# Masked Q for two heads in one K group, exp in steps of 3 and 2 banks, and zero-weight matmuls in TensorE's gaps

## Chip, cores and metric

The kernel runs on one core of a Trainium2 chip. The metric is the device time of one execution in microseconds (us). Each time quoted is a median over all of a kernel's executions, slow ones included. The program uses one core, so "slow" here only means that a run was over 1.5% above the fastest of its kernel.

Engine names in the profile: PE is TensorE (matmuls), PEld its weight loads, DVE is VectorE, ACT is ScalarE, POOL is GpSimd, SP issues the DMAs. QK stands for the score matmuls, PV for the product of the probabilities with V, and PSUM for the memory that TensorE writes its results to; the kernel uses it as eight banks of 512 fp32 columns.

## The reference, cut

One transformer block for 2048 tokens of width 512: layernorm, attention with 32 heads of 16, output projection, residual, layernorm, gated GELU FFN with 1792 hidden columns, residual. What matters here:

```python
scores = einsum("bhqd,bhkd->bhqk", q, k) * 16 ** -0.5
p = softmax(scores)            # 32 heads x 2048 x 2048 exponentials
o = einsum("bhqk,bhkd->bhqd", p, v)
h = x + (o merged) @ wo
h2 = h + (gelu(LN(h) @ w_gate) * (LN(h) @ w_up)) @ w_down
```

The 134 million exponentials run on ACT. They set the lower bound of the kernel.

## The kernel before, the parts that matter

Work is cut into 32 units: 4 chunks of 512 queries times 8 slots of 4 heads. A unit has 64 score tiles of 128 keys x 512 queries. A tile takes one PSUM bank. The four heads of a slot lie on the partitions 0, 32, 64 and 96, so QK matmuls with 32 rows each can run side by side in the array (in the trace those of one group start 0.003 us apart). Each head has 16 dimensions; the kernel pads each to 32 rows with zero weights.

A planner in the kernel's Python orders all instructions in advance from modelled durations. Each engine then runs its list in order and waits on semaphores.

```python
SLOTB = [(0, 1), (2, 3)]         # two slots of two banks for scores
PVB = 4                          # one bank accumulates P @ V
sch = Sched(P, [5, 6, 7])        # three banks for everything else ("dense")
def qk():                        # TensorE
    for st in range(NSTEP):      # 1024 steps of two banks
        yield Op("pe", 0.25, [two QK matmuls], gate=lambda: C["exp"] >= st - 1)
def exps():                      # ScalarE
    for st in range(NSTEP):
        yield Op("act", 0.9, ACTF(PT[:, p0:p0 + 2, :], pbank[:, bk[0]:bk[0] + 2, :], ACT.Exp), ...)
def pv():                        # TensorE, four matmuls side by side, then once a unit:
    ...                          # copy PVB out, transpose in fp32, normalise
```
(cut: reads, writes and ring indices)

Every eighth unit a query chunk is complete. Its output projection, second layernorm and FFN are then threaded between the exps of the next chunk. The FFN of the last chunk is the tail.

The planner makes an engine wait for its own earlier instruction whenever that one wrote the same buffer:

```python
def _waits_for(self, e, deps, extra=()):
    for (k, v) in list(deps) + list(extra):
        if k == e.name and v > e.count:   # only skips its own *current* group
            continue
        ...                               # else: wait on that semaphore, its own included
```

## Time and profile before

| | before |
|---|---|
| median time | 1202.06 us |
| span of the profiled run | 1193.7 us |
| mean granted TensorE clock | 0.707 |
| exps: first start, last end | 26.0 us, 1123 us |

The page, cut to the busy times, the granted clock in 40 slices of the span (in tenths of full speed), and the costliest groups (count, then busy us and mean ns of one, then idle time before them and its releaser):

```profile
PE 1072.0 (90%) x5442; PEld 268.1 (22%) x5499; DVE 277.8 (23%) x478; ACT 1019.5 (85%) x1102; POOL 189.5 (16%) x194
...
PEclk9799998555799955555589955555569965555589
...
L1131 ACT ACTIVATE PT<-pbank 128x1024 bf16<-128x1024 f32 x1024 | 983.5, 1023 | 99.0 <-PE pbank L1125 86.7
L1125 PE MATMUL pbank<-QT,KT 32*128 32x512 bf16 x2048 | 526.0, 519 | 80.7 <-ACT PT L1131 59.8
```

ACT is busy with exps nearly all the time, and where it isn't it waits for QK on PE. PE's clock is full only while there is dense work: the start, the three FFN stretches and the tail. Between them are quiet stretches with QK and PV alone, and there it is half.

Two quiet stretches in the windows view (start and end, length, busy time and count of each engine, granted clock, DMA):

```profile
450.00:510.00 60.00, 52.75 (x250) 11.04 (x248) 2.06 (x4) 58.03 (x62) 0.00 (x0) 0.50 0.00 1
700.00:760.00 60.00, 52.64 (x254) 11.31 (x252) 2.75 (x6) 57.27 (x62) 0.00 (x0) 0.50 0.00 1
```

PE is 88% busy here and still gets half clock. ACT is over 95% busy, so the half clock costs little. The timeline of such a stretch (start, length, engine, line, operation, count, idle before and releaser; PE only):

```profile
759.10 0.61 PE L1125 MATMUL pbank<-QT,KT 32*128 32x512 bf16 x2 [0.31 <-ACT PT L1131]
759.64 0.60 PE L1125 MATMUL pbank<-PT,VA 128*17 128x512 bf16 x4
```

From the QK pair's start to that of the PV group behind it is 0.54 us: this is what one group occupies at half clock. At full clock, in the FFN stretches of the same trace, it is 0.32 us.

### The profile page before, as it was taken

Reading aid. Unit: us, or ns where it says so; the run is one execution under the profiler, and the core shown is the slowest. Engines: PE = TensorE matmul, PEld = TensorE weight load, DVE = VectorE, ACT = ScalarE, POOL = GpSimd, SP = SyncE. Lnnn points to the kernel's source line nnn. Section 1 sums busy time; section 2 is a strip of 40 time slices with the busy share of each in tenths; the row PEclk is TensorE's granted clock in tenths of the full one; section 3 lists DMA queues with packets and bytes.
Section 4 is the critical chain, followed back from the end, with each engine's and each line's share of the span. In section 5 each row is a group of like instructions: output and inputs, shape, how many; then the busy total and the mean of one; then the engine's idle time right before and its main releaser. Section 6 shows DMA issues by size and latency. Waiting matters only on the chain.

```text
span 1193.7 us, 14797 instructions
## 1 busy us (share of the span) xinstructions
PE 1072.0 (90%) x5442; PEld 268.1 (22%) x5499; DVE 277.8 (23%) x478; ACT 1019.5 (85%) x1102; POOL 189.5 (16%) x194
## 2 busy tenths in 40 slices
PE   8899998888999988888999988888999988888887
PEld 2222222111222211111222211111222221111222
DVE  5343332000465100000356100000245300000232
ACT  4679999999888999999788999999889899999620
POOL 8500000000187000000059000000039200000000
PEclk9799998555799955555589955555569965555589
DMA  4000005000000100000000000000000000000000
GB/s 141 1 1 1 1 1 184 19 1 1 1 1 1 36 1 1 1 1 1 1 1 1 15 22 1 1 1 1 1 1 1 10 27 1 1 1 1 1 2 21
DMA packets 12848, 14.95 MB, mean 13 GB/s; under 512 B 1760, under 2 KB 11744, under 8 KB 12768
## 3 DMA queue, kind: packets, MB, share of 16 engines
q1 hardware_dynamic: 12768, 13.90, 3.5%
q8 instruction: 48, 0.79, 0.3%
q14 instruction: 32, 0.26, 0.1%
HBM read 11.80 MB, written 2.10 MB: 12 GB/s over the span
## 4 chain that ended last, share of the span: by engine, by line
PE 65%; issue 14%; ACT 14%; DVE 2%; POOL 1%; ACTq 0%; DVEq 0%
PE pbank L1125 39%; PE pbank L1124 20%; ACT PT L1131 13%; PE pbank L1323 3%; PE pbank L1365 2%; DVE OA L1319 1%; POOL xn_sb L1214 1%; PE pbank L1359 0%; PE pbank L1381 0%; ACT w_sb L1417 0%; ACTq L152 0%; DVE stats_93 L1372 0%; DVE w_sb L1418 0%; DVE QT L1254 0%; DVE h_c_69 L1368 0%
## 5 line engine op out<-in xcount | busy, mean ns | idle before, releaser
L1131 ACT ACTIVATE PT<-pbank 128x1024 bf16<-128x1024 f32 x1024 | 983.5, 1023 | 99.0 <-PE pbank L1125 86.7
L1125 PE MATMUL pbank<-QT,KT 32*128 32x512 bf16 x2048 | 526.0, 519 | 80.7 <-ACT PT L1131 59.8
L1125 PE MATMUL pbank<-PT,VA 128*17 128x512 bf16 x2048 | 270.1, 519 | 0.8 <-ACT PT L1131 0.6
L1125 PEld LDWEIGHTS pbank<-QT,KT 32*128 32x128 bf16 x2048 | 111.2, 96 | 503.6 <-PE pbank L1125 365.1
L1375 POOL TENSOR_SCALAR rstd_95<-mv_94 128x1 f32<-128x1 f32 x16 | 3.6, 222 | 907.2 <-DVE mv_94 L1373 907.2
L1319 DVE COPY OA<-pbank 128x512 f32<-128x512 f32 x32 | 22.1, 691 | 522.8 <-PE pbank L1125 522.8
L1125 PEld LDWEIGHTS pbank<-PT,VA 128*17 128x17 bf16 x2048 | 50.6, 89 | 187.1 <-issue 136.8
L1124 PE MATMUL pbank<-wd_sb,GUT 128*128 128x512 bf16 x213 | 59.2, 382 | 2.7 <-PE pbank L1125 1.0
L1411 POOL TENSOR_TENSOR w_sb<-w_sb,g_sb 128x512 f32<-128x512 f32 x42 | 56.7, 1351 | 3.5
L1409 POOL TENSOR_TENSOR w_sb<-g_sb 128x512 f32<-128x512 f32 x42 | 49.8, 1186 | 21.8 <-DVE g_sb L1407 21.7
L1323 PE MATMUL pbank<-ident_79,OA 128*128 128x128 f32 x128 | 38.9, 401 | 6.5 <-DVE OA L1319 5.7
L1418 DVE SCALAR_TENSOR_TENSOR w_sb<-w_sb,g_sb 128x512 f32<-128x512 f32 x42 | 41.9, 999 | 7.4 <-ACT w_sb L1417 7.3
L1423 ACT ACTIVATE w_sb<-pbank 128x512 f32<-128x512 f32 x14 | 8.4, 597 | 37.5 <-PE pbank L1124 37.5
L1124 PE MATMUL pbank<-xnT,wq_pad 128*128 128x512 bf16 x119 | 36.3, 384 | 1.6 <-PE pbank L1125 0.6
L1124 PE MATMUL pbank<-xnT,wk_pad 128*128 128x512 bf16 x121 | 36.6, 383 | 1.2 <-PE pbank L1125 0.5
L1407 DVE COPY g_sb<-pbank 128x512 f32<-128x512 f32 x42 | 29.0, 690 | 35.9 <-PE pbank L1124 35.8
L1443 DVE SCALAR_TENSOR_TENSOR GUT<-pbank,w_sb 128x512 bf16<-128x512 f32 x42 | 29.0, 691 | 24.5 <-PE pbank L1124 23.2
L1410 POOL TENSOR_SCALAR w_sb<-w_sb 128x512 f32<-128x512 f32 x42 | 30.5, 726 | 3.7
L1257 DVE CAST KT<-pbank 128x512 bf16<-128x512 f32 x32 | 22.1, 691 | 31.6 <-PE pbank L1124 31.6
L1254 DVE TENSOR_SCALAR QT<-pbank 128x512 bf16<-128x512 f32 x31 | 21.4, 689 | 34.1 <-PE pbank L1124 34.1
L1365 PE MATMUL pbank<-wo_sb,OnT 128*128 128x512 bf16 x57 | 24.9, 529 | 2.6 <-issue 1.7
L1417 ACT ACTIVATE w_sb<-w_sb 128x512 f32<-128x512 f32 x42 | 26.3, 626 | 0.0
(100 smaller groups left out, 484.5 us busy)
## 6 DMA issues: line engine op xcount, KB each, us to landing
xres<-in_A_x_dram SPq DMA_DIRECT2D x16, 128.0 KB, 2.3
out_dram<-out_sb SPq DMA_DIRECT2D x16, 128.0 KB, 1.7
wg_sb<-in_B_w_gate_dram SPq DMA_DIRECT2D x1, 1792.0 KB, 7.3
wu_sb<-in_B_w_up_dram SPq DMA_DIRECT2D x1, 1792.0 KB, 11.8
wd_sb<-in_B_w_down_dram SPq DMA_DIRECT2D x1, 1792.0 KB, 16.5
x_sb<-in_A_x_dram SPq DMA_DIRECT2D x3, 512.0 KB, 7.2
wqkv_sb<-in_A_wqkv_dram SPq DMA_DIRECT2D x2, 384.0 KB, 7.9
x_sb<-in_A_x_dram SPq DMA_DIRECT2D x2, 256.0 KB, 2.9
```

What stands on the lines that cost most here:

```text
L1124: return lambda e: e.matmul(o, l, r, start=start, stop=stop)
L1125: return lambda e: e.matmul(o, l, r, start=start, stop=stop, tile_position=tile)
L1131: return lambda e: e.activation(out=o, in_=i, func=func, **kw)
L1319: yield Op("dve", 0.61, lambda e: e.tensor_copy(out=OA[:, par, :], in_=pbank[:, PVB, :]), reads=[("pb", PVB)], writes=[("OA", par)])
L1323: yield Op("pe", 0.44, [lambda e, qt=qt: e.transpose(out=pbank[:, b, 128 * qt:128 * qt + 128], in_=OA[:, par, 128 * qt:128 * qt + 128], id ...
L1365: yield Op("pe", 0.44, [lambda e, hc=hc: e.matmul(pbank[:, b2, :], OnT[:, qt, hc, :], wo_sb[:, hc, :], start=(hc == 0), stop=(hc == 3)) fo ...
L1407: yield Op("dve", 0.61, lambda e: e.tensor_copy(out=gs, in_=pbank[:, b, :]), reads=[("pb", b)], writes=[("g", i)], extra=dE)
L1409: yield Op("pool", 1.05, lambda e: e.tensor_tensor(out=ws, in0=gs, in1=gs, op=ALU.mult), reads=[("g", i)], writes=[("w", i)])
L1410: yield Op("pool", 0.62, lambda e: e.tensor_scalar(out=ws, in0=ws, scalar1=GA, scalar2=1.0, op0=ALU.mult, op1=ALU.add), reads=[("w", i)], ...
L1411: yield Op("pool", 1.27, lambda e: e.tensor_tensor(out=ws, in0=ws, in1=gs, op=ALU.mult), reads=[("w", i), ("g", i)], writes=[("w", i)])
L1418: yield Op("dve", 0.6, lambda e: e.scalar_tensor_tensor(out=ws, in0=ws, scalar=1.0, in1=gs, op0=ALU.add, op1=ALU.mult), reads=[("w", i), ( ...
L1443: fn = lambda e: e.scalar_tensor_tensor(out=GUT[:, fc, :], in0=pbank[:, b, :], scalar=0.5, in1=w_sb[:, i, :], op0=ALU.mult, op1=ALU.mult)
```

## The change

Its intent: (1) fewer projections, because two heads share a 32-row K group and each Q copy is zero outside its own head; (2) fewer ACT instructions, 3 and 2 banks in turn; (3) full TensorE clock everywhere, by matmuls with zero weights ("fills") wherever the plan has a gap on PE. The banks now go 5 to scores, 1 to PV, 2 to dense work. The diff cut to its core:

```diff
-NRING = 20
+NRING = 30
+SLOTS = ((0, 3), (3, 2))
+PVB = 5
+DENSE = (6, 7)
+COLS = 3900
-    KT = at("KT", [128, NSLOT, S], BF16)
+    KT = at("KT", [128, 4, S], BF16)
 # K: one projection serves two slots; Q: one projection, two masked copies
-  op = ... tensor_scalar(out=QT[:, c, slot, :], in0=pbank[:, b, :], scalar1=0.25, ...)
+  for par in range(2):
+      ... tensor_scalar(out=QT[:, c, 2 * j + par, :], in0=pbank[:, b, :], scalar1=qmask[:, par:par + 1], ...)
 # QK and exp: a step is now n = 3 or 2 banks
-  ACTF(PT[:, p0:p0 + 2, :], pbank[:, bk[0]:bk[0] + 2, :], ACT.Exp)
+  ACTF(PT[:, p0:p0 + n, :], pbank[:, b0:b0 + n, :], ACT.Exp)
+    fill_op = Op("pe", TMM, lambda e: e.matmul(pbank[:, PVB, :], zero_bf[:], ones_bf[:], start=False, stop=False, ...), writes=[("pb", PVB)], cols=512)
+    def fill(st):                       # st: when PE's next real work is planned to start
+        if C["pv"] % NT and C["pv"] < NT * NU:
+            op = fill_op                # adds zero to the bank that PV accumulates in
+        elif sch.banks: ...             # or into a free dense bank
+        t0 = max(sch.t["pe"], sch._ready(op))
+        if st - t0 < TMM or sch.busy_columns(t0) >= COLS:
+            return False                # no gap, or 3900 columns planned in the last 3.4 us
+        sch._emit(op, t0)
```
(cut: durations of the model, keys, item lists, head order)

`busy_columns` counts a 512-column matmul on the full array as 512 and a QK matmul on 32 rows as 128. The order of the built kernel has 456 fills: 21 to 25 in each of the 16 quiet units (362 together), 14 to 23 in the unit before each run of them, 0 to 3 in each of the others, and 14 in the tail.

## The prediction

> **What bounds it now.** ScalarE, with stalls. The page has ACT busy 1019.5 of 1193.7 us, of which the 1024 exps (128x1024) are 983.5. In the trace they start every 0.92 us when nothing disturbs them: 1024 x 0.915 = 937 us. But the exps run from 26.0 to 1123.0 us, 1097 us. The missing 160 us, from start-to-start times of exps: about 20 before 90 us, 11 in the projections (90-190), 39 in the quiet units (mean 0.984, with 1.05 about one time in four and 1.5-1.7 where a unit ends and fp32 transposes run), and 85 in the three FFN stretches (22 of it are the 42 tanh between exps). The waits view names PE nearly alone: 86.7 us in 136 waits of exps on QK. The rest is the start (26 us) and the tail (71 us).
>
> The granted clock is 0.5 in all quiet stretches and for about 14-37 us into each FFN stretch; mean 0.707. Cold, a QK pair takes a slot of 0.53 us, warm 0.32. The Trainium skill (TensorE: Matmul & The Clock Gate, Part 1) says activity in windows of about 3.4 us releases the throttle; the trace agrees, its clock changes fall on multiples of 3.41 us. Weighting matmul columns by the share of the array used, I count about 1,850 per window in quiet stretches; windows kept or gained full clock from about 2,900 up.
>
> **What the change does.**
> 1. Exp of 3 and 2 banks. 0.915 = 0.062 + 2 x 0.4265, so five banks cost 2.257 us, not 2.288: 410 x 0.031 = 13 us less of pure ScalarE time. On the critical path, but small.
> 2. Fills. 456 zero matmuls by the instruction order, about 23 per quiet unit. With QK and PV that makes about 3,300 columns per window, enough on average but, as they come in clumps, not always; I expect some cold windows near unit ends. Warm PE: QK 26 x 0.33 + PV 16 x 0.33 + fills 23 x 0.3 = about 21 of 29 us, so fills fit. Gain: most of the quiet excess (39 to about 20), and each FFN stretch starts warm (non-tanh excess 63 to about 40).
> 3. Sharing K. Projections fall from 80 to 48: 128 matmuls of 0.22-0.27 us less, mostly before 195 us. Q is evacuated twice (0.69 us DVE each), K half as often. Start and projections: about 10 us.
> 4. Dense banks 3 to 2, PT ring 20 to 30. Neither should bind: DVE evacuations take 0.69 us, FFN is paced by POOL (about 3.3 us per gate). Tail, with seven free banks and a warm clock: 5 us better.
>
> **Sum.** Start 24 + exps 924 + tanh 22 + start/projection stalls 23 + quiet 22 + FFN 40 + tail 66 = 1121 if savings are partial; about 1075 if stalls nearly vanish. I predict 1100 us, 1060 to 1145. Faster by over 2%: 0.91; within: 0.05; slower: 0.04.
>
> **What would show it.** Granted clock in quiet stretches 0.85-1.0 (step 2). Exp pitch per five banks 2.26-2.32 us in quiet units (steps 1, 2), unit about 29.5 us against 31.5. PE-to-exp waits down from 87 to below 45 us. Tail at or below 67 us.
>
> **What would make it wrong.** Fills too few to hold the clock: they then run at half speed in front of QK and PE (about 2.6 us per five banks) becomes the bound: 1180-1250 us. Or full-array fills between row- and column-tiled groups costing a drain each, well over 0.3 us. Or two dense banks starving FFN so the tail grows.

## The result, and the profile after

The changed kernel takes **1262.71 us** (median of 4) against 1202.06 us: slower by 5.3%. Ratios in this document are the mean time of one kernel's fast runs over that of the other's in the same rounds, so not quite the ratio of the medians; here 1.053, with a 95% interval of 1.0475 to 1.0586.

The page after, same lines, and the fills:

```profile
PE 1138.9 (90%) x5723; PEld 276.7 (22%) x5827; DVE 259.5 (21%) x462; ACT 997.6 (79%) x897; POOL 181.7 (14%) x191
...
PEclk8899655555699995555689955555599985555599
...
L1151 ACT ACTIVATE PT<-pbank 128x1536 bf16<-128x1536 f32 (+1 forms) x819 | 959.3, 1247 | 180.6 <-PE pbank L1145 177.0
L1145 PE MATMUL pbank<-QT,KT 32*128 32x512 bf16 x2048 | 420.7, 509 | 44.0 <-ACT PT L1151 39.0
...
L1511 PE MATMUL pbank<-ones_bf,zero_bf 128*128 128x512 bf16 x386 | 226.6, 587 | 36.5 <-PE pbank L1145 21.3
```

The exps themselves took 24 us less (959.3 against 983.5), as they should. But they waited 177 us for QK instead of 86.7, the mean clock did not rise (0.708), and the fills ran at a mean of 587 ns. (Some matmul records are missing from a trace; the weight loads show all 456.)

Where the time went shows best by parts of the program. I take the start of each unit's first exp in the trace; "quiet" are the last four units of each chunk, "FFN" the first four units of chunks 1 to 3.

| us | start | units 0-3 | 12 FFN units | 16 quiet units | tail | span |
|---|---|---|---|---|---|---|
| before | 26.0 | 146.5 | 443.5 | 506.9 | 70.8 | 1193.7 |
| after | 30.1 | 136.9 | 407.3 | 616.8 | 68.9 | 1260.1 |

Outside the quiet units the change gained 44 us. In the quiet units it lost 110: 38.6 us each against 31.7. Three stretches with only QK, PV and fills, in the windows view:

```profile
150.00:210.00 60.00, 55.14 (x241) 11.33 (x242) 2.07 (x4) 47.22 (x41) 0.00 (x0) 0.50 0.00 1
435.00:465.00 30.00, 23.51 (x158) 6.77 (x160) 2.07 (x4) 30.00 (x28) 0.00 (x0) 1.00 0.08 23
750.00:810.00 60.00, 55.63 (x239) 11.23 (x242) 2.06 (x5) 47.02 (x41) 0.00 (x0) 0.50 0.00 1
```

The middle one is what the change was made for. The clock came out of the FFN at full and the fills kept it there for a while. ACT never stops (30.00 of 30.00 us). Five banks took 2.26 us between 430 and 468 us, where I had predicted 2.26 to 2.32. The other two show the state after the clock has been lost: it stays at half until the next dense work, and ACT works 47 of 60 us. Five banks take 3.05 us.

PE's timeline in the half-clock state:

```profile
229.15 0.61 PE L1145 MATMUL pbank<-PT,VA 128*17 128x512 bf16 x4
229.82 0.10 PEld L1511 LDWEIGHTS pbank<-ones_bf,zero_bf 128*128 128x128 bf16 x1 [0.58 <-PE pbank L1145]
229.83 1.27 PE L1511 MATMUL pbank<-ones_bf,zero_bf 128*128 128x512 bf16 x2
230.49 0.10 PEld L1511 LDWEIGHTS pbank<-ones_bf,zero_bf 128*128 128x128 bf16 x1 [0.56 <-PE pbank L1511]
231.03 0.10 PEld L1145 LDWEIGHTS pbank<-QT,KT 32*128 32x128 bf16 x3 [0.44 <-ACT PT L1151]
231.03 0.61 PE L1145 MATMUL pbank<-QT,KT 32*128 32x512 bf16 x3
...
231.69 1.45 ACT L1151 ACTIVATE PT<-pbank 128x1536 bf16<-128x1536 f32 x1 [1.03 <-PE pbank L1145]
```

PE has no gap. Two fills stand between PV and the QK that ACT is waiting for, and ACT is idle for 1.03 us. The second fill starts 0.66 us after the first (1.27 for two less 0.61 for one): its weight load waited for "PE pbank L1511", the fill before it.

**Theory (T1).** At half clock the fills make TensorE the bound, and the state keeps itself. Per five banks TensorE must do 2 QK groups and 1.25 PV groups of 0.54 us and about 1.8 fills, 1.75 + 1.8 x 0.6 = 2.8 us, plus the transposes at the end of a unit, against 2.26 us of exps. It therefore runs without pause, yet does not do enough to get its clock back. To see this I weight each matmul's columns by the share of the 128 x 128 array that it uses and count them in windows of 3.41 us, the raster on which the clock changes. This is a count of mine from the trace, not a view; a transpose counts as 128 columns. In the half-clock windows of this run that stayed so, the median is about 2,610. In the run without fills below, whose trace has all matmul records, the lowest count that was followed by full clock is about 3,080 and the highest that was followed by half clock about 3,020 (from 50 us to the last exp). The change's own trace lacks 104 matmul records; with these counted where their weight loads stand, its six clock rises after 30 us followed counts of 2,977 to 3,320. So saturated half-clock work of this kind lies below what raises the clock, and I take the bound for a rise as about 3,000 to 3,100. It is not sharp: five half-clock windows of 3,100 to 3,364 were not followed by a rise. Nor is the bound for a loss: the last windows before the four long half-clock stretches count 2,095, 2,539, 3,036 and 2,533, each with 3,274 or more in the window before it, but two windows of about 2,500 between 441 and 458 us kept full clock.

**Rivals.** T2: the steps of 3 and 2 banks, the masked Q or the two dense banks cause the loss, and fills only use idle time. A further question within T1 is what in a fill costs: its streamed columns, a fixed cost per instruction, or its wait for the matmul before it.

### The profile page after: what moved, and what is told of

Read it like the earlier page. It is cut to its first block, busy times and chain, and to the rows that moved or that the text cites. A ratio compares the mean times of both kernels' runs of the same rounds, so it can differ in the third digit from the quotient of the medians.

```text
span 1260.1 us, 14333 instructions
## 1 busy us (share of the span) xinstructions
PE 1138.9 (90%) x5723; PEld 276.7 (22%) x5827; DVE 259.5 (21%) x462; ACT 997.6 (79%) x897; POOL 181.7 (14%) x191
## 4 chain that ended last, share of the span: by engine, by line
PE 72%; ACT 10%; POOL 7%; issue 6%; DVE 2%; ACTq 0%; DVEq 0%
PE pbank L1145 39%; PE pbank L1511 16%; PE pbank L1144 13%; ACT PT L1151 10%; POOL w_sb L1433 3%; PE pbank L1344 2%; POOL w_sb L1431 2%; POOL w_sb L1432 2%; DVE OA L1340 1%; POOL xn_sb L1220 1%; PE pbank L1521 1%; PE pbank L1381 0%; DVE g_sb L1429 0%; DVE QT L1268 0%; ACT w_sb L1439 0%
## 5 line engine op out<-in xcount | busy, mean ns | idle before, releaser
L1151 ACT ACTIVATE PT<-pbank 128x1536 bf16<-128x1536 f32 (+1 forms) x819 | 959.3, 1247 | 180.6 <-PE pbank L1145 177.0
L1145 PE MATMUL pbank<-QT,KT 32*128 32x512 bf16 x2048 | 420.7, 509 | 44.0 <-ACT PT L1151 39.0
L1145 PE MATMUL pbank<-PT,VA 128*17 128x512 bf16 x2048 | 264.3, 506 | 2.2 <-DVE OA L1340 1.0
L1511 PE MATMUL pbank<-ones_bf,zero_bf 128*128 128x512 bf16 x386 | 226.6, 587 | 36.5 <-PE pbank L1145 21.3
L1145 PEld LDWEIGHTS pbank<-QT,KT 32*128 32x128 bf16 x2048 | 83.3, 95 | 364.4 <-ACT PT L1151 160.7
L1511 PEld LDWEIGHTS pbank<-ones_bf,zero_bf 128*128 128x128 bf16 x435 | 44.7, 103 | 216.4 <-PE pbank L1511 117.5
L1145 PEld LDWEIGHTS pbank<-PT,VA 128*17 128x17 bf16 x2048 | 50.4, 89 | 182.6 <-PE pbank L1511 68.9
L1440 DVE SCALAR_TENSOR_TENSOR w_sb<-w_sb,g_sb 128x512 f32<-128x512 f32 x42 | 35.3, 840 | 18.9 <-ACT w_sb L1439 18.6
L1144 PE MATMUL pbank<-xnT,wqkv_sb 128*128 128x512 bf16 x121 | 36.9, 391 | 2.0 <-DVE xnT L1234 0.7
L1268 DVE TENSOR_SCALAR QT<-pbank,qmask 128x512 bf16<-128x512 f32 x31 | 23.3, 751 | 8.1 <-PE pbank L1144 6.8
L1220 POOL TENSOR_SCALAR xn_sb<-x_sb,mv,rstd 128x512 bf16<-128x512 bf16 x12 | 24.8, 2076 | 0.5 <-issue 0.3
```

Of the source, the lines that this page charges most:

```text
L1144: return lambda e: e.matmul(o, l, r, start=start, stop=stop)
L1145: return lambda e: e.matmul(o, l, r, start=start, stop=stop, tile_position=tile)
L1151: return lambda e: e.activation(out=o, in_=i, func=func, **kw)
L1220: lambda e, t=t: e.tensor_scalar(out=xn_sb[:, t % 8, :], in0=x_sb[:, t, :], scalar1=mv[:, t, 0:1], scalar2=rstd[:, t:t + 1], op0=ALU.subtr ...
L1440: yield Op("dve", 0.6, lambda e: e.scalar_tensor_tensor(out=ws, in0=ws, scalar=1.0, in1=gs, op0=ALU.add, op1=ALU.mult), reads=[("w", i), ( ...
L1511: fill_op = Op("pe", TMM, lambda e: e.matmul(pbank[:, PVB, :], zero_bf[:], ones_bf[:], start=False, stop=False, skip_group_check=True), re ...
```

## The experiments

Twelve kernels ran. All gave correct results.

### e1: no fills

```diff
-    sch.fill = fill
```

> The change without any zero-weight matmul, all else kept. Theory T1 (at half clock the fills make TensorE the bound): quiet stretches stay at granted clock 0.5, but five banks of exp take 2.35 to 2.45 us there instead of 3.05, and the time falls to 1140 to 1175 us, below the kernel before. Rival T2 (the 3-and-2-bank steps, the masked Q or the two dense banks cause the loss, and the fills only use idle TensorE time): the time stays at 1240 us or more, five banks at 2.9 us or more. Rival T3 (both share the loss): 1190 to 1230 us.

Measured: **1109.47 us**, ratio 0.925 to before (0.920 to 0.930). Clock 0.719, half in the quiet stretches as before:

```profile
410.00:530.00 120.00, 98.61 (x530) 20.71 (x530) 5.49 (x12) 116.72 (x104) 0.00 (x0) 0.50 0.00 1
```

PE fell to 82% busy at the same half clock, and ACT rose to 97%. The exps' wait for QK fell from 177.0 to 41.8 us (total, times, longest):

```profile
ACT PT L1151 <- PE pbank L1145: 41.8, 55, 5.2
```

A quiet unit takes 29.8 us (477.4 / 16). Without its fills the change would have been 7.5% faster than the kernel before. T2 falls, and T1 holds: 139 us of the quiet units' 617 come from about 360 fills, 0.39 us each. It was even faster than my range.

### e2 and e10: more fills

```diff
-COLS = 3900
+COLS = 5200      # e2; e10: 4400
```

> The change with the fill budget raised from 3900 to 5200 columns in 3.4 us: 719 fills instead of 456, about 36 per quiet unit. T1 with the reading that the clock was lost because too few columns came in a window: granted clock near 1.0 in the quiet stretches, five banks at 2.26 to 2.33 us, 1070 to 1110 us. If more fills can't hold the clock either, each is paid at about 0.6 us: 36 x 0.6 us more per quiet unit, 1330 to 1450 us at clock 0.5. T2: no better than 1240 us whatever the clock.

> Between the change (3900, 456 fills) and e2 (5200, 719 fills): 602 fills, about 30 per quiet unit, self-waits kept; about 3,700 columns per window at full clock. If the clock is a matter of columns per window with a bound near 3,000, most windows pass but some may not: runs at 1085 to 1100 us where it holds and 1150 to 1300 us where it is lost in a stretch, so more scatter from run to run than e1 or e7. If the number of fills mattered smoothly, all runs near 1175.

Measured: e2 (719 fills) **1095.82 us**, ratio 0.913; three runs at 1094 to 1097 with a clock of 0.99, one slow at 1174.14 with a clock of 0.897. e10 (602 fills) **1077.99 us**, ratio 0.894; three runs at 1075 to 1079 with a clock of 0.99, one slow at 1148.85, clock 0.897. The clock by slices in e10's profiled run:

```profile
PEclk9699999999999999999999999999999999999999
```

So the change with 456 fills is 60 us slower than before, and with 602 fills it is 124 us faster. This is no smooth dependence on their number; it is whether the clock is held. Quiet units take 29.0 us in e10 and 29.8 in e2: at full clock, fills beyond what is needed cost again. The slow runs, some 75 us longer, show that neither is safe. (They were not profiled; that they lost the clock in a stretch is read from their mean clock.)

### e3 and e9: two heads in each K group, but 2-bank steps and no fills

```diff
-SLOTS = ((0, 3), (3, 2))
-PVB = 5
-DENSE = (6, 7)
+SLOTS = ((0, 2), (2, 2))
+PVB = 4
+DENSE = (5, 6, 7)      # e9: (5, 6)
-    sch.fill = fill
```

> Two heads in each K group alone: exp steps of 2 and 2 banks as before, three dense banks, no fills. T1: 1150 to 1185 us, 5 to 20 us over e1. T2 with the 3-and-2-bank steps as the cause: clearly faster than e1, 1150 to 1180 us against 1240 or more for e1.

> e3 (2-bank steps, no fills) with its dense banks cut from three to two, so that against e1 only the exp steps differ. If the two dense banks cost nothing, 1180 to 1200 us like e3, and the 80 us between e3 and e1 belong to the steps of 3 and 2 banks (at half clock five banks then need 2 QK slots of 0.53 us, not 2.5). If two dense banks are what helped e1, well below 1180.

Measured: e3 **1189.67 us**, ratio 0.986 (0.977 to 0.995), one of four runs (1195.14) slow. e9 **1196.61 us**, ratio 0.996 (0.989 to 1.003). By the medians of the same rounds, e3 gains 12 us on the kernel before and e9 6; by the intervals, e3 gains 6 to 28 us and e9 anything from a gain of 14 to a loss of 3. So the shared K, with the longer PT ring and the new order that come with it, is worth little, and the third dense bank (e3 against e9) is not told from nothing, for the two intervals overlap. Between e9 and e1 only the exp steps differ, and that is 87 us (from different rounds, with the kernel before at 1202.78 and 1202.03 us). I had expected 5 to 20 us between e3 and e1. In the units: quiet 31.7 each in e9 against 29.8, FFN units 446.5 together against 397.9. So 29.5 us of the 87 lie in the quiet units and 49 in the FFN units. By the prediction's estimate only some 13 us are ACT's own time. The exps' wait for QK is 91.9 us in e9 and 41.8 in e1, so QK has a large share: at half clock a QK group occupies PE for 0.54 us whether it has two or three matmuls, so a unit needs 25.6 of them instead of 32, and every second refill has the longer exp of 3 banks to hide behind. In the FFN units the clock differs too: its mean is 0.80 in e9 and 0.89 in e1. The measured difference is shown; its causes are argued from the durations, and no run separates them.

### e4: 2-bank steps with fills, both states in one run

As e3, with the fills kept (budget 3900, 555 fills).

> As e3 with the fills on at the same budget of 3900: 555 fills, 29 per quiet unit. T1: the same two states as the change has. If 29 per unit hold the clock, quiet clock over 0.9 and 1085 to 1120 us; if not, 1260 to 1340 us at clock 0.5. T2: within 20 us of e3.

Measured: **1271.94 us**, ratio 1.060; one run slow at 1338.15. Its profile has both states, from the same instructions. Two windows of quiet units:

```profile
560.00:640.00 80.00, 78.17 (x288) 14.79 (x287) 1.42 (x4) 58.58 (x58) 0.00 (x0) 0.50 0.00 1
840.00:920.00 80.00, 75.31 (x440) 20.93 (x436) 2.75 (x6) 80.00 (x89) 0.00 (x0) 1.00 0.00 1
```

58 exps in 80 us, or 89. The units take 44.8 us in the first and 29.3 in the second. In the first, PE is 98% busy for 80 us and its clock stays at half. This is the plainest evidence that being busy is not what raises it, and that the state holds itself.

### e5: fills of 128 columns

```diff
-pbank[:, PVB, :], zero_bf[:], ones_bf[:], start=False
+pbank[:, PVB, 0:128], zero_bf[:], ones_bf[:, 0:128], start=False   # and alike for free banks
```

> The change with each of its 456 fills cut from 512 to 128 columns; number, place and order of the instructions the same. If the loss is the columns streamed at half clock, the fills shrink to about a third of their cost: clock 0.5 in quiet stretches (about 2,300 columns per window at most), five banks at 2.4 to 2.55 us, 1120 to 1150 us. If the loss is a fixed cost for each fill (weight load, change between tiled and full array, wait for the matmul before), little is saved: 1200 to 1260 us.

Measured: **1150.72 us**, ratio 0.958, clock 0.5 in quiet stretches. The 16 quiet units take 514.4 us, 37 more than without fills: 0.10 us a fill, against 0.39 with 512 columns. With a quarter of the columns a fill costs about a quarter: the cost goes with the columns streamed, and these two runs show no fixed part beside it.

### e6: fills that do not wait for TensorE's own semaphore

```diff
 if op.eng == "pe":
     P.group_end("pe")
+    if getattr(op, "isfill", False):          # set in fill()
+        fn_, w_, s_, d_ = P.eng["pe"].ops[-1]
+        P.eng["pe"].ops[-1] = (fn_, [w for w in w_ if w[0] != "pe"], s_, d_)
```

The Trainium skill (TensorE: Matmul & The Clock Gate, Part 3) says that matmuls start and end in program order. I infer that a matmul need not wait for an earlier one that writes the same bank.

> The change with one thing taken out: a fill no longer waits on TensorE's own semaphore for the matmul before it ([...]the check finds no race). In the trace of the change fills in a row stand 0.66 us apart at half clock and 0.45 at full, not 0.43 and 0.22. If this wait is what makes the fills fill up TensorE at half clock, the pitch falls to 0.43 to 0.54 and the time to 1130 to 1200 us, and the clock may climb back by itself (then 1085 to 1110). If the wait is not what matters, 1240 to 1265 us.

Measured: 1156.4 us over all four runs, two of which (1161.74 and 1162.67) count as slow; the fast ones are at 1143.02 and 1151.07, ratio 0.954. Same 456 fills as the change. Two fills in a row now start 0.40 us apart at half clock (median of 88 pairs in the trace) instead of 0.66 (the median in the change). The clock by slices:

```profile
PEclk9899886868699996785999995656689995979799
```

It is lost as before, but it comes back after 3 to 41 us each time, many times in the run. With the cheaper fill, TensorE at half clock gets more done: by the count above, the median of the half-clock windows that stayed so is about 2,840 instead of 2,610, and it is granted full clock again.

### e8 and e7: no TensorE instruction waits for TensorE

```diff
-            if k == e.name and v > e.count:
+            if k == e.name and (v > e.count or k == "pe"):
                 continue
```

> e1 (no fills) with no TensorE instruction waiting for TensorE's own semaphore: what the waits cost without fills. 1098 to 1110 us, at most 10 us under e1, at clock 0.5 in quiet stretches.

> e2 (budget 5200 columns) with no TensorE instruction waiting for TensorE's own semaphore. Full clock held in all runs, fills in a row 0.22 us apart, quiet units 28.9 to 29.2 us instead of 29.8: 1070 to 1085 us. If the fills' self-waits cost nothing: as e2, 1094 to 1097.

Measured: e8 (no fills) **1089.13 us**, ratio 0.906. Against e1's 1109.47 that is 20 us, twice what I expected; in the profiled runs the tail has the largest share of it (61.6 us against 69.1). e7 (5200 columns, 719 fills) **1063.17 us**, ratio 0.884 (0.882 to 0.886), all four runs within 4 us and none slow. Its quiet stretch:

```profile
410.00:530.00 120.00, 102.58 (x699) 28.74 (x712) 10.64 (x23) 120.00 (x107) 1.20 (x4) 1.00 0.00 1
```

and fills in its timeline:

```profile
483.56 0.82 PE L1511 MATMUL pbank<-ones_bf,zero_bf 128*128 128x512 bf16 x3
484.58 0.39 PE L1145 MATMUL pbank<-QT,KT 32*128 32x512 bf16 x3 [0.20 <-ACT PT L1151]
```

ACT is busy 120 of 120 us. Three fills take 0.82 us where one takes 0.39: a fill each 0.215 us, and QK comes in time (PE waits for ACT, not ACT for PE).

### e12: the same with fewer fills

COLS = 4400 with e8's edit.

> e10 (budget 4400, 602 fills) without any wait of TensorE on its own semaphore: the search for a version that holds the clock with fewer fills than e7. If the smaller cost of a fill makes recovery possible, all runs at 1052 to 1066 us and none slow. If 30 fills per quiet unit are too few when TensorE is faster, some runs lose the clock for a stretch: 1070 to 1130 us and a mean clock of 0.85 to 0.95.

Measured: **1063.26 us**, ratio 0.881 (0.878 to 0.885), four fast runs at 1059 to 1064. Between the start and the tail its profiled run lost the clock twice, for 3 and 7 us, and got it back each time; e7's did so once, for 7 us. e7 and e12 are equal within noise, and both beat both kernels: 12% under the kernel before.

### e11: the kernel before without TensorE's self-waits

> The kernel before with only TensorE's waits on its own semaphore left out. e8 against e1 gained 20 us (1.8%) by this; here 1170 to 1190 us is expected, with the clock pattern unchanged. If the gain needs the new exp steps or the masked Q, 1195 to 1205.

The edit is e8's, in the kernel before. Measured: **1173.63 us**, ratio 0.974 (0.966 to 0.981, a gain of 1.9 to 3.4%); clock still half in the quiet stretches. The waits cost the old kernel some 29 us too (1202.78 us in the same rounds).

## Why the prediction was wrong, point by point

The prediction said 1100 us and faster with a chance of 0.91. It was 1262.71 and slower.

- **What bounds the kernel** was right: ACT with stalls caused by QK on PE. e10, e7 and e12, in which ACT runs without pause in quiet units, take 1063 to 1078 us.
- **Step 2, the fills, is the step that failed.** The prediction says: "about 3,300 columns per window, enough on average but, as they come in clumps, not always; I expect some cold windows near unit ends", and of the time on PE: "so fills fit". I took a lost window as a local cost of a few us, after which the average counts again. But the 3,300 presuppose full clock. Once it is lost, the fills and groups take twice as long, TensorE saturates, and its rate is what half clock permits (median about 2,610), below the bound for a rise. The average was right: the eight windows from 441 to 468 us, at full clock, have a mean of 3,260. One short window thus cost the rest of the quiet stretch: 150 to 201 us at half clock four times over, at 3.05 us per five banks. I named this case under what would make it wrong, with 2.6 us per five banks and 1180 to 1250 us, but gave "slower" a chance of 0.04. The numbers to see it were there: 2.6 us of TensorE work against 2.26 us of exps says that the half-clock state saturates, and in the trace of before, with PE 28.40 of 30 us busy from 840 to 870 us, the windows of that stretch counted 1,632 to 2,954 and the clock stayed at half. The margin was also smaller than I took it to be: I set the bound at about 2,900, but with the 57 matmul records that this trace lacks put back, the lowest count there that was followed by full clock is about 3,100.
- **A fill's cost** was mis-sized. I used 0.3 us at full clock; in a row they stood 0.45 us apart there and 0.66 at half clock, because each waited for the matmul before it on TensorE's own semaphore. That wait is visible in the planner's code. I had not looked for it. e6 shows that with this wait gone the same fills take 0.40 us at half clock and let the clock return.
- **Step 1, the exp steps,** was right in ACT's own time (five banks at 2.26 us where undisturbed, 2.257 predicted; its 0.4265 us a bank agrees with the trace of before, where a 1024-column exp takes 1.023 us and a 512-column ACTIVATE from PSUM 0.597) but sized at 13 us. Without fills it is worth 87 us (e9 to e1), probably in large part because of QK's slots on TensorE, which I had not costed.
- **Step 3, shared K:** about 10 us predicted for start and projections. The change gained about 6 there, and e1, without the fills, 12. Over the whole run e9 and e3 gain 6 and 12 us, near the noise.
- **Step 4:** e9 with two dense banks is 7 us above e3 with three, which is within the noise, so that they bind is not shown. The tail went from 70.8 to 68.9; predicted 66.
- The FFN stretches gained 36 us, against 23 plus about 5 for the exps in the sum. That this comes near is luck: I had put it down to fills that keep the clock for the start of each stretch, and e1, without any fill, gained 46 us there.

So the gain that I expected exists, and more: 93 us without any fills (e1). The fills at this budget gave back 153 us.

What stays open: where exactly the bounds for the clock lie, since my count of columns fits its rises only roughly and its losses badly; and why single runs of e2 and e10 lost the clock.

## What to carry to other kernels

Work added to keep an engine's clock up has two prices, and the one at the low clock decides: if the added work saturates the engine there, a single short window can hold it down for the rest of the stretch, so check that the low-clock state either has slack or does enough to climb out. Measure the kernel without the helper first; here the helper hid a 7.5% gain. And look for an in-order engine that waits on its own semaphore: taking these waits out gained 15 to 33 us in four pairs of kernels here, and with fills none of the eight runs of e7 and e12 was slow. (In e6, where the fills alone no longer waited, two of four were.)

## What the Trainium skill lacked or had wrong

- "TensorE: Matmul & The Clock Gate", Part 1, says that a busy window of about 3.4 us releases the throttle. The trace agrees with the raster of 3.41 us, but not with "busy": in e4 TensorE was busy 78.17 of 80 us and stayed at clock 0.50. The page does not say that matmuls on part of the array count for less; with columns weighted by the share of the array, the bound in e1 lies between about 3,020 and 3,080 columns per window (other traces show it less sharp).
- The same page has no word on a state that keeps itself: extra matmuls at half clock that saturate TensorE and still do not raise it (e4: 44.8 us a unit against 29.3 for the same instructions).
- The same page, Part 3, states that matmuls complete in program order. No page gives the cost of a wait on TensorE's own semaphore: 0.66 against 0.40 us from fill to fill at half clock (the change, e6), 0.45 against 0.215 at full clock (the change, e7).
- "TensorEngine Tiling (Array Packing)", Key Properties, says that a change of tiling mode drains TensorE, without a figure. Here a QK or PV group of 512 columns between groups of another tiling occupies 0.32 us at full clock and 0.54 at half, against 0.215 for a fill behind a fill at full clock: an estimate from these of about 0.1 us for the change. TensorE's waits on its own semaphore are not the reason: in e8, without them, a QK group occupies 0.53 us at half clock and 0.315 at full.
- "ScalarE: Activation LUTs", What ACT_TABLE_LOAD costs, gives 186 ns plus 0.833 ns a column for an ACTIVATE with immediate scale and bias, less an overlap of 93 ns: an estimate of 0.946 us for 1024 columns. The undisturbed exps of the kernel before start every 0.90 to 0.92 us.
